# Scaling nine weight tiles in place, with their low halves on GpSimd, under a new order table

## The chip, the cores and the metric

The kernel runs on one core of a Trainium2 chip. The metric is the device time of one execution in microseconds (us), the median of several runs. The engines are TensorE (matmuls; PE in profile rows, PEld for its weight loads), VectorE (DVE), ScalarE (ACT), GpSimd (POOL) and the DMA queues, of which the kernel issues through SyncE (SP) and ScalarE.

## What is computed

An attention with 2 batches of 8 heads, 768 positions and head size 64, in which a query sees only the keys of its own hash bucket, then two feed-forward blocks over 1536 tokens of width 512:

```
q_bits = einsum(q, proj) > 0;  k_bits = einsum(k, proj) > 0      # 6 bits: the bucket
scores = where(bucket(q) == bucket(k), q @ k.T / 8, -1e9)
x = softmax(scores) @ v                                          # heads side by side: 1536 x 512
h = max(x @ w1, x @ w2, x @ w3);  x = h @ w_out                  # first MoE,  512 -> 768 -> 512
h = x @ w_in;  x = where(h > 0, h, exp(min(h, 0)) - 1) @ w_out2  # second MoE, 512 -> 2048 -> 512
```

The weights arrive as 64-bit floats and q, k, v in 32 bits.

## The kernel before

Nearly every product is done in 16 bits with two halves: a number is scaled by a power of two, its rounded high half and the remaining low half are both kept in 16 bits, and three matmuls (high x high, high x low, low x high) stand for one product of 32 bits.

The attention is cut into 96 tiles of 128 queries against 768 keys, four to a pair of heads (a unit). Each tile has score matmuls (`scores`, L621), a maximum (L624), scale and bias (L625, L627), an exponential on ScalarE (L629), the two halves of its result (L658 or L660, and L664), a transposing DMA (L666) and 18 matmuls with the values (L672 to L674). The first 16 tiles stay in 32 bits and transpose on TensorE (L641, L645, L650). Queries and keys are loaded in blocks, scaled in place (L396 or L397), split into halves (L398, and L400 on GpSimd or VectorE) and transposed on TensorE (L410).

The first MoE's three weight matrices are cut into six column blocks f = 0..5, so 18 tiles of 128 x 512. `plan_w13(f)` (L574 and following) loads three of them through `plan_w` into `raww` (L531), turns 64 into 32 bits in `dc2w` (L535 to L546; six buffers), finds the scale of the three from a product of the tiles with themselves (`gram`, L297 to L301, then `pow2`, L318 and L320) and splits each with `plan_wsplit`: the scaled high half on ScalarE (L558) or VectorE (L559), then the low half on VectorE (L560). The second weight of the first MoE and the weights of the second go the same way. The products of both MoEs are at L713 (`mm3`) and L848.

None of the instructions is issued in the order of the program text. `Graph.op` only notes each operation with the engines on which it may run, and `Graph.emit` issues them in the order of `ORDER`, a packed table of one entry per operation: its number and the engine that takes it. Each engine then works through its own entries in that order; DMAs are entries of the SP queue (D) or of ScalarE. The cost figures and `prio` values that stand beside the operations are not used when the kernel is built; the keys of an operation's dictionary are only the engines that the table may choose.

```
        todo = [(hi << 8 | lo) for lo, hi in zip(raw[:n], raw[n:])]
        for t, w in enumerate(todo):
            o, e = self.ops[w >> 3], ENGINES[w & 7]
            assert e in o["eng"] and all(place[d] < t for d in o["deps"])
            o["fn"](e)
```

Of the kernel before, what the change touches and what calls it, by code (L numbers as in the profile page):

```python
# [30 lines left out]
class Graph:  # L31
# [73 lines left out]
    "c-lQyOITXx))u_6@y5m*8*gm9vC$at$|h<6O~OWvfLG8cV48~QKx_wMG7y`A*bKyzf!Gejb|AI`@pK@z1F;>5?LbTiVmlB|2I9#;Ob3#a|9Sqk&H4Yezi)l-`>uDb4UgNcWz6SqKV$!(5=mvVN=j#N"  # L105
    "UYZxbaC_pfyb0VH#K#-Q{hL!L@yD)|EQI>ufz@F1o3Y)KSzPaUb6yn;&OCQ6#%A5uPUiA=F1Li6?m6)kt}A@s`|GDDxx3zQy0__k`*)Pktj44}ISg~}>3gp*<Qw!iGxo@|sC-`@Q!JXP_>nHIxOP*_"
    "Roys4;5BgO2-XzyrGa()oa>XK<R4~Lxc8|EI}ljad@;UnBlI%6^yj&H^Wo2!Qu8#Vo)4?^$Ajj`nQkc>NxwSwYa@oM^Xr)5<jv$~%S=CJet`#PhOHjtEoUn5s|h=ro!;|W@x8w$dEq%b?pO%!FK+mj"
    "jf9(3>+yuV&Mn`%EOrszj_*Z&R52#^FqUg;o{R3!U?F@3f8jFCi@%xwT^e?~E`Ih{CB%yjw?`r;HWya+13O+)9Xi;FD%7^{*}KR~Dzc`~z0$Q`gmw)Rp)0fPa^eU3kMZ}D_9eH>G2==2O1Y#N_D(NQ"
    "{-3qR1fAm-<E+zVUNIRQJF5tSPPn6-#a_?GyKM}!e7MHlfvrioIT+fb7@H?ZU;;hWJ?C4mt+orZpp1;$ncFtw<+JpFSRDMFm<%bcClb6`T6JbmVE&tOIQ7WV(BJ3^3sVZe4L;_e;zK$1Lmh4ttHao-"
    "?r68UmJ`Jd5!Ibqk(n2qpcb^!_PJO{WD|xB&z72xH_uRW#4X{!u*Rp5W&E4f8O9g07oIP#7ffC+xv8jq=kr^acNEcp?ZA$IKzVx}bx8c%OI$vGqMMu}V&*?wYf|r}L+&<DM?P$L3|k4#^*LqdKUC`Y"  # L110
    "{DrS$g0ZmfUqt+i+(2&}^Bu$z74DgD#;K##F{AER+s2=p>|=v#-C~b8u$?yx*XB~+p`P)I`60@6ZT@PlKKlANwu2oEBH@2du+YeN=Letr&-wlUH;DYAeSWkWGf3WFGxwJni70YLoJ;WqvPvm8Cs;jG"
    "u9Nyp<;=gltn?Wl6^ifdeu*02vV!7uJ}P)A(XeJqi3u4z0^vneY%W~2oeerJS9F}c=>N=zH>AIj2xYE4vu<PW7XQGVE{q5WKln*m?V!@Fx3x#tf+}KW)lk>zF?oNSQ^n-I!*lP1ukA;FLhM4ecN}+r"
    "rRr2O77w)J2KFoD^|fuAnH1JU%zr7OcE|1l#nmNr8e*1$;32YfJ@qwOhHbDI<Hu7z;j`!3H}8?nIrO{8DHpzNU?Q*`3|c-HXvLQXGr^YDJr}LTIkM#=Wq^0}x;d!F(2!bcJrPXcx~i>X$(eyvp4jRa"
    "?c#sQm~Ot=bB<3Kl(UKJ-m~x3Z^hAtS*iB#tr*vK&M-Vnm}Y#4O}*L~CMPdDf8oSmFzhn61Djp=fd5X^uDTX2PM7?Lr*5xlL352TeLd@b>t5TijdieWN71ykxlK>!>%lGmJa)ueuf@6B$G9R;y&Q=6"
    "ep4*`b?6Tkm=glgnCHM-7Sd|0val^;bg^cLZ^CtRzRk<%?>jNc-uGOk{67?5_f=e$q*XD-5t+^SD)gu2h4x5fus>CE-<;}H)V8s7))ZJ-Fld6WywheZv}S&c=t?KX7mgE7BGu98GIBM(_(eQ68<E<k"
    "#N?TBaR#L@caLz@BQ`9$PnW$O-bVEAt@G%Vv#xnLcI?@Zc)ZVizMh>IyK!cGkM$dlV*A=@gW2jhy>#L`zZ^xUeiE}yJFaWH)pl)XeEEmsvi8p0@5JswobeLj3jTSF%tzLJ{=hZk5Yc7-u@a7Oc?cd|"
    "Kt)nQd$8&MN4vT(%9km><(Do}N4jqU$HD4aGW_Q9eUi~ElPRwRM+)lc7lgEp95l}(d@DM$st}&fO5jEQx#b6^+O4muce&&1(;lr!wHc>QHX;ni*0R&!GP{1VT5VGk$GvZ*9xwIl=d4rT4vM{+`4Sh`"
    "`tMw>Jdf_3GIhq6yl8CI8)vf5V*+9?7?&N*4l?%5R-H}44uvDx@acbBnNeT0&lO67e@r{bRj*R^m5+N!>7y^zMrDC_Oe+Y#I{Vh}u58o4=U@C!;C%5jG<Xz?9}@=(DMjiG39qOAVozUN!VJWGysSp~"
    "I)hn+|7&((-c{xHJUyMrS#*267avY1?QiSXCsZ3YhqEIA*;?N6Y##g3!Jo{RJD1OAF=6D_XlxMPrYz4d?^g-w??-$4X4`kyOpev-^V=AqnP<D<Nc4OU3)VK{bBZ)sOcGbVsG2_@O@~VAD~5jElf!<+"
    "^Sw4M>Tqh@A2=YS=+w;EXV|+hk1pd3guC$P@?Ww^_(QmS%r7k?J*TtI9g+Qw%k6dS8!gpqPd6^VupXT{m!{8s(VyMdN(Lg3IHvi#zF<fz6DbDa{+)l<QnO}j?q6rot9bV3%;kFJ=KRvC+^gBvjT-~6"  # L120
    "PFTSi(@W2!6@7i$+#dDDSu4IB>aE*@$!xe@H4|ePh$XLXH#p;X6AHg)a`?5Di&^};sw;&-6B&;)=3V>C!&`?o`xUa~XKTzB4tI4!Hx!=GPtIX>#Cz)C1rGMMaUu{r$G6<#NHi8>bYB0UcLol_Qjgzj"
    "BSik7GXX(sNuvcjJUNSKjS@6!iOF4lYd{+H*?7yA_txb^59<RvwzlE(Zv}-0R57UDvrh%Z6H+ps#KeR;htp(ToDkZMR_4}}#txB`ocH?XkEdMP9ouvyI%9EgX8FRwE2m|`{>w2T-G@iY<|OSoj<X$)"
    "*XMqQF8zAp)WuKdT&|T(43D|vd*=s7S8OFUFLvSNwx8NFd}e}&<3ve#!=B*8lx_9s#O^r#F`#xc5W7QiaYfF|@tqr6ucc@HFBStXkH8gYh-(jm9Cr30&R-{AD|bR6O1HJ+6xBuo!R7N4<-v(uNu3TJ"
    "g?U%ebG_j`1Bo4TBiQ)Vlr^>;2!;c}(`fwtjKfJ>z7H{$m<Xyw+?ERo;zThVpPb<f<}j!0>(#_EDXL=_<SO`m9NUzecJ`z)6@hu;nxM`rTKP5<{@3=naPQ!{nrWbPQh371b4$oN6DGFU<n$aesfhd="
# [24 lines left out]
    "q^D<ebU;7SKQPd*H<@~RU_sMB|3H6FfB%4fz(~UZI%qzk8yFqv83h8K!Ty24!NCE8(J-JJ>>nK*06IGOG2k?e8b%-+2H+T=(ZJy7kO68&gK=<VXw+mJ932@onM}q3qtO5{3MS*A(P%Uo45k5a!7|YO"  # L149
    "M#Ip^2+ioy(8!R%1dbtK#=#-O&=8bIM~8-nhK-}ckWF;SU>q`;hH3F8nShz-!#MnZ@#xVbxVd@gruWgK;bGH9c@%WukD%ib)B%}>>GJRmel$ww5gLt*n$6}%77M`P(NPl+v&C$I7&bpPJvNUF12LP&"  # L150
    "Kpc5O7tEG1^GD4*cH<s1kByC4Ml6q^=P@7)%^zDH10Ngv1UQXB8vEoioUk81f%@Z5pf>gd(x;z(0u}Il^2r$NC$K+x0unUbp#RrEd_tR_JbCiz6B<3C5uG1DfytkK`sw)ilW}@m=z~U2{!gRHm<0$3"
    "H`k4u&QEU2k3YSM{{=r07MT"
# [821 lines left out]
```

## Time and profile before

| | us |
|---|---|
| median of three runs | 646.44 (646.3 to 650.33) |
| the profiled execution | 646.06 |
| its span, first to last instruction | 644.3 |
| TensorE busy | 624.7 |
| VectorE busy | 528.0 |
| ScalarE busy | 454.8 |
| GpSimd busy | 218.5 |

A page of the profile gives, for one execution, the busy time of each engine, the chain of work that ended last, and groups of like instructions. A row of instructions reads: line of the kernel, engine, operation, output<-inputs, output shape and type<-input shape and type, count. The difference between an execution's time and its span, 1.8 us here, lies around the first and last instruction. In a time line, a bracket at the end of a row gives the idle time of that engine just before and what ended it. Busy time counts overlapping instructions of one engine once.

### The profile page before, as it was taken

The numbers are of one execution on the slowest core, as the hardware profiler recorded it, in microseconds if no ns is written. First come the engines' busy times: TensorE is split into PE (matmuls) and PEld (weight loads), VectorE is DVE, ScalarE is ACT, GpSimd is POOL, SyncE is SP. The second block draws the span as 40 slices with busy tenths as digits, with TensorE's granted clock in tenths as the row PEclk, the third lists the DMA queues.
The fourth block names the chain that finished last, engine by engine and source line by source line (L and its number), as shares of the span: only waits on it lengthen the run. The fifth ranks groups of instructions, "written<-read, shape, count | busy, mean of one in ns | idle before, by whom it ended". The sixth has DMA issues, their size and how long they took to land.

```text
span 644.3 us, 16489 instructions
## 1 busy us (share of the span) xinstructions
PE 624.7 (97%) x6414; PEld 490.8 (76%) x6414; DVE 528.0 (82%) x1493; ACT 454.8 (71%) x858; POOL 218.5 (34%) x196
## 2 busy tenths in 40 slices
...
GB/s 261 200 242 152 180 202 229 217 131 218 150 189 178 149 156 164 174 169 151 147 132 218 181 96 128 68 99 35 97 19 71 45 1 2 1 1 2 1 92 105
DMA packets 176030, 81.35 MB, mean 126 GB/s; under 512 B 142672, under 2 KB 170320, under 8 KB 175952
## 3 DMA queue, kind: packets, MB, share of 16 engines
...
## 4 chain that ended last, share of the span: by engine, by line
PE 80%; DVE 4%; ACT 4%; DMA 3%; issue 1%; POOL 0%; DVEq 0%; SPq 0%; ACTq 0%
PE mo L713 47%; PE out L848 19%; PE s L621 6%; PE o L672 2%; PE o L673 2%; PE o L674 2%; ACT P L629 1%; DVE m L624 1%; DMA kb<-ka 1%; DMA rawv<-in_v_dram 1%; PE mo L410 1%; DMA PT<-hl 1%; ACT hl L645 1%; DVE hx L734 0%; ACT mo L535 0%
## 5 line engine op out<-in xcount | busy, mean ns | idle before, releaser
L713 PE MATMUL mo<-xT,w 128*128 128x256 f16 x1296 | 152.6, 272 | 0.0
L664 POOL TENSOR_TENSOR hl<-P,hl 128x768 f16<-128x768 f32 x69 | 115.0, 1674 | 64.9 <-ACT hl L658 31.5
L713 PEld LDWEIGHTS <-w 128*128 128x128 f16 x1296 | 123.6, 98 | 16.7
L713 PE MATMUL mo<-x1T,win 128*128 128x256 f16 x1152 | 135.8, 273 | 0.0
L848 PE MATMUL out<-wo2t,gt 128*128 128x512 f16 x576 | 134.9, 379 | 0.0
L713 PEld LDWEIGHTS <-win 128*128 128x128 f16 x1152 | 112.3, 98 | 24.2
L629 ACT ACTIVATE P<-s,bias,scale 128x768 f32<-128x768 f32 x96 | 94.6, 991 | 28.8 <-DVE bias L627 17.6
L841 POOL TENSOR_TENSOR gt<-g,gt 128x256 f16<-128x256 f32 x57 | 39.3, 695 | 213.2 <-ACT gt L839 125.4
L624 DVE TENSOR_REDUCE m<-s 128x1 f32<-128x768 f32 x96 | 91.1, 951 | 12.6 <-PE s L621 11.2
L848 PEld LDWEIGHTS <-gt 128*128 128x128 f16 x576 | 54.9, 97 | 52.7
L832 ACT ACTIVATE r<-mo,nih 128x256 f32<-128x256 f32 x96 | 44.8, 469 | 69.1 <-PE mo L713 65.0
L835 DVE TENSOR_SCALAR uu<-e,sg 128x256 f32<-128x256 f32 x96 | 35.5, 371 | 26.3 <-ACT e L834 25.7
L658 ACT CAST hl<-P 128x768 f16<-128x768 f32 x62 | 50.7, 830 | 2.9 <-DMA PT<-hl 2.4
L672 PE MATMUL o<-vt,PT 128*128 128x65 f16 x480 | 51.3, 193 | 0.2
L673 PE MATMUL o<-vt,PT 128*128 128x64 f16 x480 | 51.3, 194 | 0.0
L674 PE MATMUL o<-vt,PT 128*128 128x65 f16 x480 | 51.1, 192 | 0.0
L837 DVE SCALAR_TENSOR_TENSOR g<-mo,aj,uu 128x256 f32<-128x256 f32 x96 | 46.1, 482 | 6.0 <-POOL gt L841 2.0
L621 PE MATMUL s<-ka,qa 128*128 128x384 f16 x192 | 48.1, 332 | 2.5 <-ACT P L629 1.9
L621 PE MATMUL s<-kb,qb 76*128 76x384 f16 x192 | 48.2, 332 | 1.0 <-DMA kb<-ka 1.0
L672 PEld LDWEIGHTS <-PT 128*128 128x128 f16 x480 | 44.4, 96 | 2.7 <-DMA PT<-hl 0.4
L673 PEld LDWEIGHTS <-PT 128*128 128x128 f16 x480 | 44.3, 97 | 2.1
L713 PEld LDWEIGHTS <-wot 128*128 128x128 f16 x432 | 41.4, 98 | 5.6
...
## 6 DMA issues: line engine op xcount, KB each, us to landing
...
```

The lines of the kernel that those rows point to most:

```text
L621: PE.matmul(ps.ap[:, h, :NK], lh[0:n, h0 + i, j], rh[0:n, i, h * CH:(h + 1) * CH], start=first, stop=not first)
L624: op({"V": vred(S)}, lambda e: V.tensor_reduce(out=m.ap, in_=ps.ap[:, :, :NK], op=ALU.max, axis=AX.XY), rd=[ps], wr=[m], prio=t + 80.5)
L629: op({"A": act(S, ap=2, acc=int(u < FU)) - 42}, lambda e: A.activation(out=P.ap.rearrange("p (c n) -> p c n", c=2), in_=ps.ap[:, :, :NK], ...
L658: A.copy(hl.ap[:, 0], P.ap)
L664: op({"G": gtt(S), "V": (vtt(S), -109.46)}, lambda e: eng[e].tensor_tensor(out=hl.ap[:, 1], in0=P.ap, in1=hl.ap[:, 0], op=ALU.subtract), r ...
L672: PE.matmul(oo, pt.ap[:, kt], vt.ap[:, i, kt, :D + 1], start=(kt == 0), stop=False)
L673: PE.matmul(oo[:, :D], pt.ap[:, kt], vt.ap[:, i, kt, D + 2:], start=False, stop=False)
L674: PE.matmul(oo, pt.ap[:, NS + kt], vt.ap[:, i, kt, :D + 1], start=False, stop=(kt == NS - 1))
L713: PE.matmul(o, lh(kk, x), rh(kk, y), start=(kk == 0 and pi == 0), stop=(kk == n - 1 and pi == 2))
L832: op({"A": act(NQ, ap=1) - 42}, lambda e, m=m, o=o, r=r: A.activation(out=r.ap, in_=o.ap[:, :NQ], func=AF.Relu, scale=nih.ap[:, m:m + 1]), ...
L837: op({"V": vstt(NQ)}, lambda e, m=m, o=o, uu=uu, gg=gg: V.scalar_tensor_tensor(out=gg.ap, in0=o.ap[:, :NQ], scalar=aj.ap[:, m:m + 1], in1= ...
L848: PE.matmul(outs[j].ap, gt.ap[:, x, j * 128:(j + 1) * 128], wo2t[f].ap[:, y], start=(len(seen) == 1 and pi == 0), stop=(len(seen) == n and ...
```

## The change

`plan_wsplit` gets a second form, which `plan_w13` uses for f = 0, 1, 2, so for nine of the 18 tiles. In it the tile in `dc2w` is multiplied by its scale in place, the high half is a plain copy of it, and the low half is a subtraction of two tiles in SBUF that GpSimd can do.

```diff
-    def plan_wsplit(tag, t2, dst, dfn, s, prio):
+    def plan_wsplit(tag, t2, dst, dfn, s, prio, pool=False):
         w = lambda: t2.ap.bitcast(F32)
+        if pool:
+            op({"A": act(512, ap=1), "V": vts(512)}, lambda e: A.activation(out=w(), in_=w(), func=AF.Copy, scale=s[1]())
+               if e == "A" else V.tensor_scalar(out=w(), in0=w(), scalar1=s[1](), scalar2=None, op0=ALU.mult), rd=[t2, s[0]], wr=[t2], two=True, prio=prio)
+            op({"V": vcopy(512), "A": act(512)}, lambda e: (V.tensor_copy if e == "V" else A.copy)(dfn(0), w()), rd=[t2], wr=[dst], two=True, prio=prio)
+            return op({"G": gtt(512), "V": vtt(512)}, lambda e: eng[e].tensor_tensor(out=dfn(1), in0=w(), in1=dfn(0), op=ALU.subtract),
+                      rd=[t2, dst], wr=[dst], two=True, prio=prio)
...
-            wops.append(plan_wsplit("w", t2[i], f"w13{f}{i}", lambda x, i=i: w13[:, f, i, x], s, prio))
+            wops.append(plan_wsplit("w", t2[i], f"w13{f}{i}", lambda x, i=i: w13[:, f, i, x], s, prio, f < 3))
```

Two cost figures of DMA entries change by one (1200 to 1201, 900 to 901, 100 to 101 on ScalarE's queue), which has no effect on what is built. `ORDER` is replaced as a whole: 3368 entries instead of 3359. Unpacked in the way of `emit`, the two tables hold the same operations but for the nine tiles, in another order and partly on other engines. The larger shifts between engines, in numbers of entries:

| operation | before | after |
|---|---|---|
| nine tiles: scaling in place | none | 5 VectorE, 4 ScalarE |
| nine tiles: high half | 4 VectorE, 5 ScalarE | 5 VectorE, 4 ScalarE |
| nine tiles: low half | 9 VectorE | 9 GpSimd |
| attention, high half (L658, L660) | 62 ScalarE, 18 VectorE | 54, 26 |
| attention, low half (L664) | 69 GpSimd, 11 VectorE | 64, 16 |
| first MoE, low half of its result (L770) | 10 GpSimd, 2 VectorE | 5, 7 |
| second MoE, low half (L841) | 57 GpSimd, 39 VectorE | 45, 51 |
| small copies of the hash bits to 16 bits (L453 to L459) | 20 ScalarE, 8 VectorE | 13, 15 |

GpSimd's own order begins, after the new table: key block 1, query block 2, key block 2, two weight tiles of f = 0, query block 4, key block 3, the third weight tile of f = 0, query block 6, two weight tiles of f = 1, and so on; before, the same without the weight tiles.

## Rows read from the trace of the kernel before

**Rows 1.** The page's head: span, and busy time of TensorE (PE) and its weight loads.
```profile
span 644.3 us, 16489 instructions
...
PE 624.7 (97%) x6414; PEld 490.8 (76%) x6414; DVE 528.0 (82%) x1493; ACT 454.8 (71%) x858; POOL 218.5 (34%) x196
```
**Rows 2.** Busy time by stretch: bounds, length, then us (instructions), clock, DMA share, GB/s.
```profile
core 0: us, PE busy (x) PEld busy (x) DVE busy (x) ACT busy (x) POOL busy (x), PEclk, DMA share, GB/s
0.00:32.00 32.00, 22.33 (x253) 18.70 (x254) 23.91 (x85) 19.47 (x36) 6.16 (x19) 1.00 0.76 231
32.00:64.00 32.00, 31.28 (x372) 27.51 (x369) 31.34 (x90) 32.00 (x61) 3.83 (x3) 1.00 0.66 197
64.00:91.34 27.34, 22.99 (x191) 18.66 (x191) 25.75 (x69) 26.46 (x45) 10.95 (x9) 0.94 0.77 193
91.34:128.00 36.66, 36.54 (x506) 31.20 (x504) 35.98 (x98) 36.63 (x58) 24.86 (x16) 1.00 1.08 216
128.00:640.00 512.00, 511.13 (x5098) 394.73 (x5096) 409.75 (x1154) 340.23 (x662) 172.67 (x150) 1.00 0.46 105
```
**Rows 3.** TensorE's instructions in order of time: start, length in us, instruction, [idle before].
```profile
40.20 0.50 PE L410 MATMUL mo<-ident,natk 128*128 128x128 f16 x6
...
86.87 0.84 PE L621 MATMUL s<-kb,qb 76*128 76x384 f16 x2
...
90.69 0.48 PE L621 MATMUL s<-ka,qa 128*128 128x384 f16 x2
...
91.34 1.47 PE L713 MATMUL mo<-xT,w 128*128 128x256 f16 x12
```
**Rows 4.** The chain of waits between 70.99 and 90.69 us, shares by line.
```profile
by line: ACT P L629 30.7%; issue 17.9%; ACT hl L645 13.4%; ACT mo L535 8.9%; ACT hl L658 8.6%; ACT dc2w L539 5.3%; ACT w L558 4.5%; ACT vt L500 3.7%; ACT qa L413 2.8%; ACT xn L696 2.0%; ACT rawq L396 1.3%; ACT junk L333 1.0%
```
**Rows 5.** VectorE's, then ScalarE's instructions in order of time.
```profile
48.48 0.48 DVE L559 TENSOR_SCALAR w<-dc2w,swm 128x512 f16<-128x512 f32 x1
48.87 0.75 DVE L560 SCALAR_TENSOR_TENSOR w<-dc2w,swm,w 128x512 f16<-128x512 f32 x1
49.53 0.46 DVE L540 TENSOR_SCALAR dc2w<-raww 128x512 uint16<-128x512 uint16 x1
...
53.37 0.73 ACT L558 ACTIVATE w<-dc2w,swm 128x512 f16<-128x512 f32 x1
53.98 0.99 ACT L629 ACTIVATE P<-s,bias,scale 128x768 f32<-128x768 f32 x1
```
**Rows 6.** Groups by line and shape: count | busy us, mean ns | idle before, releasers.
```profile
L396 ACT ACTIVATE rawq<-rawq,sq 128x512 f32<-128x512 f32 x4 | 2.9, 720 | 0.8 <-DVE sq L320 0.8
...
L398 DVE TENSOR_SCALAR natq<-rawq 128x512 f16<-128x512 f32 x12 | 6.0, 501 | 0.1
...
L743 ACT CAST hTb<-hx 128x512 f16<-128x512 f32 x4 | 2.4, 608 | 0.0
...
L745 POOL TENSOR_TENSOR hTb<-hx,hTb 128x512 f16<-128x512 f32 x9 | 11.6, 1291 | 24.0 <-DVE hTb L743 11.4 <-PE mo L281 6.7 <-ACT hTb L743 3.2
```
**Rows 7.** GpSimd's instructions in order of time.
```profile
35.68 1.66 POOL L400 TENSOR_TENSOR natk<-rawk,natk 128x768 f16<-128x768 f32 x1 [2.67 <-DVE vs L320]
60.15 1.16 POOL L400 TENSOR_TENSOR natq<-rawq,natq 128x512 f16<-128x512 f32 x1 [22.82 <-DVE scale L625]
```
**Rows 8.** Busy time by stretch, up to tile 6's scores and on to tile 28's.
```profile
0.00:38.59 38.59, 28.63 (x357) 24.23 (x358) 30.06 (x101) 26.06 (x49) 8.82 (x20) 1.00 0.76 233
38.59:114.48 75.89, 71.11 (x768) 60.45 (x766) 73.93 (x207) 74.98 (x126) 25.40 (x18) 0.98 0.80 197
```
**Rows 9.** One line each: count: min/median/max ns, first to last start.
```profile
L397 DVE TENSOR_SCALAR rawq<-rawq,sq x8: 473/486/1074, 5.3 to 271.9; 128x512 f32<-128x512 f32 x8
...
L398 DVE TENSOR_SCALAR natq<-rawq x12: 409/421/1280, 5.9 to 272.5; 128x512 f16<-128x512 f32 x12
...
L400 POOL TENSOR_TENSOR natq<-rawq,natq x10: 1152/1171/1817, 17.9 to 273.0; 128x512 f16<-128x512 f32 x10
```
**Rows 10.** VectorE's instructions on the first chunk's weights, in order of time.
```profile
30.75 0.15 DVE L320 TENSOR_SCALAR swm<-swm 128x1 int32<-128x1 int32 x1
...
38.06 0.74 DVE L560 SCALAR_TENSOR_TENSOR w<-dc2w,swm,w 128x512 f16<-128x512 f32 x1
```

More of the change, by code (lines that the diff above doesn't have):

```diff
@@ L104 @@
 ORDER = (
[L105 to L124, printed above, removed]
@@ L149 @@
[L149 to L152, printed above, removed]
+    "c-l2qOF$au+7`Sqcw_Jecw_JecnNrA&=|n$;Ell>U{pYpi0wj57h<yzn}ygc#AYFB7h<~*dltcV5lj|hyAYFw*et|$Atnp)bP+sVh^LGH9ee(FzWKiQeV*riK1OB+ON3IHlFlT^C;COls%h@ePx&gg"
@@ new lines @@
+    "%k7DIeH=_Ajr$zI#nS12z28$l56?Y83Gxs%=`Gfymm!|-<09s`i0-Yreh4gFFQ7~Giqu6%ex38wB~i?|e<b7%@+=b7zpT3;)Fz<-U#*PBXg9l3xq^wi<hl()iL*SWph7*(^D2YugM`LfW0<znQX=ky"
+    "UB30bEqKMUlcxl^vgLov<$JeQy(hjuZ^SPQe}(<mv<tm&@X4Y683#-FZ&V~@pk~X)5nKMNEbHWy%jH@XOgd)ztj?rfS9W3Z?$68~yH`h=1d%gKbT_vA=E~~aJ2x);9Xec`b%~Ju=9Bxe&v%0de=e+G"
+    "p{JrCPqQBmMP@%7g*T%&C5zHQm1ZR_@*hIWw6!hkP0qLL@AoYq=yUobw~<au@w!$+mgiw4ay2WpZTY!&@jSZ2diM@@U~dA~ODxf;d)Z0nV%wshxT~&hH^X4Gd1|D);cu0)$d1YqRlnM|lHd6kLW^(C"
+    "-*!1j%~R*GYxAeQKu~|6*ZtMCX$pBv5ex172Mcp+$9m!2u-mSFHSKT5At+Zt{QQc%CiOQvUkilhCg&GE*Yq|TzOI>@vA?p?{eid@Ul4IDIb>+typ#LoX_xD}g?E0EbuQpM7VBx>zcFDNr*KuDDxKkq"
@@ new lines @@
+    "R`Gvr>M)c2-<H2z?m3~yVLo=vF)Xz^%?l^tFW03{jp*^=>8_iLeI;&I&W0n`9?OMS`-?t$MM!tgK3-i%Xo~2w#ip%y-W6Z$M!)Qj%_E2OSC{_7&!ueRo&d4fGp$FVHXAMcDMovX96rx~zi_lZ=Q(jN"
+    "Eyb^-;t`o+`5U$}yu3+7yI$O^Zu7r8X$$g5!!cL1?|kVpd3|nwfLHvx%T52U=c3Z|*@0m7WAKw`GbF_=wC9}T?dup@q}8hxrj65=yAsBZgt(yLJ1D83BYHL=A@%4N^FNxcwhzdb<=1tu-NAF8Mb>0d"
+    "k81zV&DXKVzjht(cy|RU{D8)%p^HPV{iP=rb<Vf?Ph69d$#`#>)6b!cs~avZX0~{?55)8KOh*louVcu9g3v2J+cX%mY*?GxUf7Pl;`>AkOXnW1Lv-T1*ms`SMx`4vN%%5G3w)0&pXIB%WbHjn)qi4N"
+    "M~I`ppKA?Kl)JTascAdWdk%Lme_1{3B43{ReI<I+%x~8_CR$vAKfqTXGvLn0(Pif(XZ`a(LK;2$!=Lb-ZEq`x9=?drB&8yW-aI{bEmO$?-c_MxhlZd^^6`yp;UmxOIrACg1R`YC=C-3dzfG%8&K+FA"
@@ new lines @@
+    "NjNe!Gr*gdD5K=Bb*2kZt>x+o{;7G9rJUm~MtA+Qn02*VW;57{8@f8hp<6o$YS&Gcch<NNg0Ad+xhS5y@06~58@@QWRM-}lvc7iXf73a~TVBoyR`ZErnDm`R{W03pe?_ii+duulWbdLIw8Nt)ZyixQ"
+    "=YR63^D=inFA+)I9xvCoydR7mcG2Y6^H=`B@!!azTO`#uoOtC+xk2f}M8AJ@X?ob9>EG7(H_f&4T-j44K^hiU-|35GR$H7|IO}qo;St$VX;8;8T%4Zx?4_wPvgi?r*EUb0zAzbaxc)e^?bsdD*6q2^"
+    "zF63+jegrj9_W8E22C?o+sTFHta(@R!*gNe=1O{Y^-Ba-Mq~4g75b`+{^luvFQyK-!|%2cG@tJ6S!cP0!H`D5^LX|D-6i&4r^?_(bC{ClTK@OjsL8UWm|Kv3_1^3AFCG%dGU~&U)9?_mkz>x$GbQFw"
+    "oXmzfqrVd*TW=Og@oTddi>$ATY_vs(bMe#Ev|jm{*@f`1W&U627rc{?(ha=TT4~$dcG_<|J6`Ah%u&KcD7@^9T)AG)KNh@seh>^j>1uVjocvGg720dUz3u)^V(@tDj8^Zi<?MCjCO)d!`!z;~ca2SG"
```

63 lines of the change are left out of this document (37 added, 26 removed).

## The prediction

> **What bounds the kernel now.** I read the page's head first, then the busy time of the engines stretch by stretch, then the chain of waits, then the instructions in order of time. The head shows TensorE busy for 624.7 of a span of 644.3 us [rows 1], so 19.6 us of waiting are all that can be had without faster or fewer matmuls, and the change removes none. The table by stretch shows where those 19.6 us are [rows 2]. From the first matmul of the first MoE at 91.34 us on [rows 3], TensorE is busy for 36.54 of 36.66 and for 511.13 of 512 us: 1.0 us of idleness in 549. The rest lies before it: 9.7 us in the first 32 us, 0.7 us up to 64, 4.35 us between 64 and 91.34; and 3.8 us in the tail, where the last sums leave. So the end of the kernel moves one for one with the time at which TensorE becomes dense, and a faster engine behind 91.34 us is worth nothing unless TensorE waits for it.
>
> What holds TensorE up before 91.34? From 32 to 128 us ScalarE is busy for 32.00 of 32, 26.46 of 27.34 and 36.63 of 36.66 us, VectorE for 31.34, 25.75 and 35.98: both are full. GpSimd, with 3.83 and 10.95 us up to 91.34, is nearly free [rows 2]. The chain of waits between 70.99 and 90.69 us names ScalarE in every piece but its own issue time, the exponentials alone with 30.7%, and no VectorE [rows 4]. The bound of this stage is ScalarE first, VectorE close behind.
>
> **The change part by part: the nine tiles.** Before, a weight tile costs one scaled copy to the high half and one VectorE instruction for the low half. By the old table the nine tiles of f below 3 have the high half four times on VectorE and five times on ScalarE. After it, a tile costs a scaling in place, a plain copy to the high half, and a subtraction; the new table puts the scalings on VectorE five times and on ScalarE four, the copies likewise, and all nine subtractions on GpSimd.
>
> Instructions overlap a little on their engine, so the price of one is the distance of two starts. On VectorE a scaled copy starts at 48.48 (0.48 us long), the low half behind it at 48.87 (0.75 long), the next instruction at 49.53: 0.39 and 0.66 us, each 0.09 less than its length. On ScalarE a scaled copy starts at 53.37 and the next at 53.98: 0.61 us [rows 5]. For the scaling in place the nearest rows are the same operation on the queries: 720 ns on ScalarE [rows 6], like the scaled copy's 0.73, so 0.61 us; a median of 486 ns on VectorE [rows 9], so 0.39 us. For the plain copy they are 608 ns on ScalarE [rows 6], so 0.50, and 421 ns on VectorE [rows 9], so 0.33 us.
> VectorE: before 4 x 0.39 + 9 x 0.66 = 7.5 us; after 5 x 0.39 + 5 x 0.33 = 3.6 us; 3.9 us saved.
> ScalarE: before 5 x 0.61 = 3.1 us; after 4 x 0.61 + 4 x 0.50 = 4.4 us; 1.4 us lost.
> GpSimd: a subtraction of this size takes 1291 ns in the mean [rows 6] and 1.16 us undisturbed [rows 7]: 10 to 12 us more, for which there are 22.8 us of idleness before 60.15 us alone [rows 7].
> The extra hop from engine to engine that each tile makes costs nothing, as long as it ends before the first matmul that reads these weights, at 91.34 us [rows 3]: the new table has the ninth subtraction ahead of the scores of tile 13 already. Without that cover it would cost its length once, the copy and the subtraction, 0.5 + 1.2 us.
> Alone, then, the change helps the engine that is second and burdens the one that is first. What comes of it hangs on the table.
>
> **The new table.** I counted the entries of both tables, each with its mean from the view of instructions by line, in two parts: up to the scores of tile 6, which start at 38.59 us in the trace, and from there to those of tile 28, at 114.48 us; TensorE has the same work ahead of either within 1 us. Up to tile 6 the new table has 3.6 us more for ScalarE (33.6 against 30.0), 0.6 more for VectorE, 0.8 for GpSimd. Between the two it has 84.0 instead of 84.9 us for ScalarE, 88.8 instead of 91.7 for VectorE, 34.3 instead of 25.4 for GpSimd. The old sums of 84.9 and 91.7 stand for 74.98 and 73.93 us of busy time [rows 8], since lengths overlap; so the differences are worth 0.9 x 0.88 = 0.8 us on ScalarE and 2.9 x 0.81 = 2.3 us on VectorE. The 3.6 us that ScalarE gets earlier (26.06 / 30.0 of it, 3.1) lie in the first 38.59 us, where it is idle for 38.59 - 26.06 = 12.5 us [rows 8]; if that cover failed they would cost their 3.1 us. So the table pays ScalarE's new passes out of its idle start, and the crowded stage becomes shorter by 0.8 us if ScalarE binds, by 2.3 if VectorE does. I take 1.2 us, nearer to ScalarE's, since the chain is ScalarE's [rows 4].
> Behind tile 28 the new table has 18 us more for VectorE, 8 less for ScalarE and 22 less for GpSimd: halves of the attention and of the second MoE go from GpSimd to VectorE. VectorE is busy for 409.75 of the last 512 us [rows 2], so 18 us fit into 102 idle ones: 0, and at worst about 1.5 us, if they crowd in one place. The loads in the SP queue change places too (one query load goes to ScalarE's queue, a weight load moves up behind the third); the first query and the first two key loads, which the first scores need, keep theirs: 0.
>
> **Against it: GpSimd beside VectorE.** VectorE's conversion of the queries has a median of 421 ns and a worst case of 1280, and GpSimd's subtraction for them a median of 1171 and a worst case of 1817 [rows 9]: now and then a pair holds each other up. Over all twelve conversions the mean is 501 ns [rows 6], 80 above the median. The ten new VectorE instructions at 80 ns lose 0.8 of the 3.9 us; I take that as covered, since ScalarE binds. The bounds are 0, if all go like the medians, and the 5.2 us of the blocking rival below.
> The Trainium skill (SBUF — State Buffer, Who interferes with whom) says that GpSimd and a VectorE instruction that uses its second port, or has two inputs in SBUF, shut each other out for a whole instruction. By that rule the worst cases above are such blocks; the medians show that most instructions here met none.
>
> **The sum.** The profiled execution took 646.06 us, 1.8 more than its span of 644.3; the median of the runs is 646.44. 646.44 - 1.2 + 0 + 0 = 645.2 us.
>
> **The rivals.**
> No gain: the early ScalarE work isn't ready early, since its weights have still to land, and its passes fall into the full stage after all; its 0.8 us are eaten. For it: ScalarE is full from 32 us on [rows 2]. Against it: 12.5 us are free before [rows 8]. 646.4.
> Blocking: each of the nine subtractions holds a waiting VectorE instruction for half of its 1.16 us, 5.2 us against 3.9 saved; VectorE is then 1.3 us longer and binds: 647.7. The medians speak against it [rows 9].
> More than forecast: the two full engines both come out ahead, and TensorE's 4.35 us of idleness between 64 and 91.34 close [rows 2]. For it: the granted clock is 0.94 in that stretch [rows 2], and a pair of score matmuls takes 0.84 us at 86.87, behind an idle time, where it takes 0.48 at 90.69 [rows 3]; less waiting gives some of this back too. 646.4 - 4.4 = 642.0.
> Slower: GpSimd's queue is in order, and the new table puts two weight subtractions ahead of those of a query block and of the fourth key block, which starts at 35.68 us now [rows 7]. The first chunk's scale is there at 30.9 us, but its first low half starts at 38.06, since VectorE is late [rows 10]. If GpSimd's first starts at 38.06 too, then two weights and the query block, 3 x 1.16 us, put the key block to 41.5. Its subtraction ends at 37.34 and its transposes run at 40.20, so it can start 2.9 us later, at 38.6, before it decides [rows 3, 7]. From there each microsecond comes out at the end: 41.5 - 38.6 = 2.9 us, 649.3; and over 652.9, if the scale comes another 3.6 us late. Against it: the new table places that scale earlier than the old one.
>
> **Chances and range.** Forecast 0.42 (644.2 to 646.4), no gain 0.20, blocking 0.08, more than forecast 0.18, slower 0.12. From 641.5 to 649.5 the range takes in the first three, most of the fourth and the near half of the fifth. One per cent, 6.5 us, is about what a measurement of this kernel can tell from no change: below 640.0 lies 0.05 (the fourth, with a gain in the first 32 us besides), above 652.9 lies 0.07 (the fifth's far half and what I have not thought of), between them 0.88.
>
> **What would show it.** Right: nine GpSimd subtractions of 1.16 to 1.3 us, ended by about 70 us; nine of VectorE's low halves left; the first matmul of the first MoE near 90 us; TensorE idle for about 3 us between 64 us and it, and for no more than 1.5 behind it. Wrong: the fourth key block's subtraction starting behind 38.6 us; VectorE's conversions with a median well above 421 ns; ScalarE as idle in the first 38 us as before; TensorE waiting behind 128 us, where VectorE got its 18 us.

## The result, and the profile after

The changed kernel takes 650.9 us in the median of 19 runs (648.48 to 655.61), the kernel before, beside it on the same chip, 646.7 us (19 runs, 642.99 to 650.33). The ratio is 1.0067, with a 95% interval from 1.0046 to 1.0089: 4.2 us slower. Forecast were 645.2 us. The time lies within 1% of the kernel before, where the forecast had put it, but on the other side of it and above the range.

The profiled execution of the changed kernel is its slowest, 655.61 us. A second profiled execution took 650.24 us, near the median, and where the two differ both are shown. Lines moved: what was L621, L629, L664, L666, L672 and L713 is now L627, L635, L670, L672, L678 and L719. The new form of a tile is L559 (scaling on ScalarE), L560 (on VectorE), L561 (copy) and L562 (subtraction).

Head of the page, and the busy time by stretch, in the columns of [rows 2]:

```profile
span 653.5 us, 16490 instructions
...
PE 630.4 (96%) x6414; PEld 495.2 (76%) x6414; DVE 534.0 (82%) x1524; ACT 451.0 (69%) x849; POOL 204.9 (31%) x183
```

```profile
0.00:32.00 32.00, 23.90 (x258) 19.60 (x258) 23.41 (x84) 20.88 (x36) 5.99 (x18) 1.00 0.81 262
32.00:64.00 32.00, 31.18 (x340) 27.78 (x340) 27.74 (x84) 28.73 (x53) 11.28 (x9) 1.00 0.52 157
64.00:91.34 27.34, 24.74 (x219) 20.66 (x219) 26.68 (x78) 27.31 (x50) 12.81 (x11) 1.00 0.70 190
91.34:128.00 36.66, 35.14 (x462) 29.36 (x461) 33.96 (x92) 35.13 (x55) 22.45 (x15) 0.95 0.91 210
128.00:640.00 512.00, 506.33 (x5098) 393.36 (x5096) 416.38 (x1178) 337.64 (x657) 150.19 (x128) 1.00 0.46 105
```

In the first row the clock column says 1.00, though matmuls ran at half rate up to 37.7 us (rows below): the trace's record of the clock begins with its first rise, at 37.74 us here and 28.80 in the kernel before, and the column counts what lies ahead of it as full.

The last line is the news. Behind 128 us, where [rows 2] have TensorE busy for 511.13 of 512 us, it is busy for 506.33: 5.7 us of idleness where 0.9 were. VectorE is busy for 416.38 us there, 6.6 more than before and far from full. The waits of TensorE behind 128 us, in the kernel before, then in the first and the second execution of the changed one (line, releaser, us in total, times, longest):

```profile
PE mo L280 <- ACT junk L333: 0.5, 1, 0.5
PE s L621 <- ACT P L629: 0.3, 1, 0.3
```

```profile
PE o L678 <- DMA PT<-hl: 4.2, 4, 2.2
PE mo L719 <- DVE hx L744: 0.8, 1, 0.8
PE s L627 <- ACT P L635: 0.6, 1, 0.6
```

```profile
PE o L678 <- DMA PT<-hl: 5.7, 3, 2.8
PE s L627 <- ACT P L635: 1.2, 2, 1.0
PE mo L719 <- DVE hx L744: 0.8, 1, 0.8
```

What TensorE waits for in the changed kernel is the transposing load of a tile's halves (PT from hl), ahead of that tile's product with the values; the kernel before has 0.8 us of such waits in its second execution and none of 0.1 us or more in its first. The nine weight tiles themselves, in the second execution (groups by line and shape):

```profile
L562 POOL TENSOR_TENSOR w<-dc2w,w 128x512 f16<-128x512 f32 x9 | 11.1, 1249 | 12.3 <-ACT w L561 6.0 <-DVE w L561 4.4 <-DVE swm L320 1.8
...
L559 ACT ACTIVATE dc2w<-dc2w,swm 128x512 f32<-128x512 f32 x4 | 2.9, 736 | 0.0
L561 ACT CAST w<-dc2w 128x512 f16<-128x512 f32 x4 | 2.4, 637 | 0.0
L560 DVE TENSOR_SCALAR dc2w<-dc2w,swm 128x512 f32<-128x512 f32 x5 | 2.4, 474 | 0.0
L561 DVE CAST w<-dc2w 128x512 f16<-128x512 f32 x5 | 2.1, 415 | 0.0
```

Their lengths are those that the prices were made from: 1249 ns on GpSimd against 1291 in [rows 6], 474 and 415 on VectorE against medians of 486 and 421 in [rows 9], 736 and 637 on ScalarE against 720 and 608.

Where the time lies along the kernel, by three marks that every version has: the starts of the 1st, the 241st and the 1321st of the 2880 matmuls of `mm3`, which makes the products of the first MoE and the first product of the second, and the time from the last of these to the end of the span. The new order puts other work ahead of the first mark than the old one; behind the third all are alike.

| profiled execution | 1st | 241st | 1321st | from there to the end |
|---|---|---|---|---|
| before | 91.3 | 142.4 | 343.2 | 301.1 |
| before, second execution | 92.4 | 144.7 | 345.7 | 301.1 |
| changed | 91.0 | 145.7 | 352.0 | 301.5 |
| changed, second execution | 85.3 | 138.5 | 346.8 | 301.5 |
| new order up to 140 us, old order behind | 85.1 | 138.2 | 340.3 | 301.1 |
| the same with the old form of the tiles | 91.0 | 144.2 | 346.2 | 301.2 |
| changed, two transposing loads earlier | 86.5 | 139.7 | 343.4 | 301.5 |
| old order, new form of the tiles | 96.4 | 149.5 | 351.2 | 301.4 |
| before, two transposing loads later | 90.1 | 141.3 | 352.3 | 301.1 |

In its second execution the changed kernel reaches the 241st matmul 6.2 us earlier than the kernel before in its second, and the 1321st 1.1 us later. The gain is made, and more than lost again between 138 and 347 us.

### The profile page after: what moved, and what is told of

It reads as the page before. It is cut to its first block, busy times and chain, and to the rows that moved or that the text cites. A ratio compares the mean times of both kernels' runs of the same rounds, so it can differ in the third digit from the quotient of the medians.

```text
span 653.5 us, 16490 instructions
## 1 busy us (share of the span) xinstructions
PE 630.4 (96%) x6414; PEld 495.2 (76%) x6414; DVE 534.0 (82%) x1524; ACT 451.0 (69%) x849; POOL 204.9 (31%) x183
## 4 chain that ended last, share of the span: by engine, by line
PE 74%; DMA 4%; DVE 4%; ACT 2%; issue 1%; POOL 1%; SPq 0%; DVEq 0%; ACTq 0%; POOLq 0%
PE mo L719 43%; PE out L854 19%; PE s L627 6%; DMA PT<-hl 4%; PE o L678 2%; PE o L679 2%; PE o L680 2%; ACT P L635 1%; DVE m L630 1%; PE mo L410 1%; ACT junk L333 1%; ACT wot L564 0%; PE mo L297 0%; PE mo L431 0%; DVE hx L740 0%
## 5 line engine op out<-in xcount | busy, mean ns | idle before, releaser
L719 PE MATMUL mo<-xT,w 128*128 128x256 f16 x1296 | 155.2, 274 | 0.8 <-DVE hx L744 0.8
L719 PEld LDWEIGHTS <-w 128*128 128x128 f16 x1296 | 124.1, 98 | 18.7 <-issue 0.9
L719 PE MATMUL mo<-x1T,win 128*128 128x256 f16 x1152 | 135.1, 273 | 0.0
L854 PE MATMUL out<-wo2t,gt 128*128 128x512 f16 x576 | 133.4, 379 | 0.0
L670 POOL TENSOR_TENSOR hl<-P,hl 128x768 f16<-128x768 f32 x64 | 106.7, 1673 | 82.8 <-ACT hl L664 45.9
L719 PEld LDWEIGHTS <-win 128*128 128x128 f16 x1152 | 112.1, 98 | 22.7 <-issue 0.2
L635 ACT ACTIVATE P<-s,bias,scale 128x768 f32<-128x768 f32 x96 | 94.3, 989 | 31.0 <-DVE bias L633 22.6
L847 POOL TENSOR_TENSOR gt<-g,gt 128x256 f16<-128x256 f32 x45 | 32.2, 718 | 225.5 <-ACT gt L845 80.1
L841 DVE TENSOR_SCALAR uu<-e,sg 128x256 f32<-128x256 f32 x96 | 34.7, 364 | 28.6 <-ACT e L840 28.2
L678 PE MATMUL o<-vt,PT 128*128 128x65 f16 x480 | 50.9, 193 | 4.2 <-DMA PT<-hl 4.2
L627 PE MATMUL s<-ka,qa 128*128 128x384 f16 x192 | 48.2, 333 | 3.0 <-ACT P L635 2.3
L664 ACT CAST hl<-P 128x768 f16<-128x768 f32 x54 | 44.6, 826 | 7.7 <-DMA PT<-hl 7.2
L678 PEld LDWEIGHTS <-PT 128*128 128x128 f16 x480 | 44.4, 97 | 7.1 <-DMA PT<-hl 4.9
L627 PE MATMUL s<-kb,qb 76*128 76x384 f16 x192 | 48.4, 334 | 0.0
L719 PEld LDWEIGHTS <-wot 128*128 128x128 f16 x432 | 41.6, 98 | 5.4
```

The source lines that it names most:

```text
L627: PE.matmul(ps.ap[:, h, :NK], lh[0:n, h0 + i, j], rh[0:n, i, h * CH:(h + 1) * CH], start=first, stop=not first)
L635: op({"A": act(S, ap=2, acc=int(u < FU)) - 42}, lambda e: A.activation(out=P.ap.rearrange("p (c n) -> p c n", c=2), in_=ps.ap[:, :, :NK], ...
L664: A.copy(hl.ap[:, 0], P.ap)
L670: op({"G": gtt(S), "V": (vtt(S), -109.46)}, lambda e: eng[e].tensor_tensor(out=hl.ap[:, 1], in0=P.ap, in1=hl.ap[:, 0], op=ALU.subtract), r ...
L678: PE.matmul(oo, pt.ap[:, kt], vt.ap[:, i, kt, :D + 1], start=(kt == 0), stop=False)
L719: PE.matmul(o, lh(kk, x), rh(kk, y), start=(kk == 0 and pi == 0), stop=(kk == n - 1 and pi == 2))
```

## The experiments

**Both kernels again, one execution each.**

> The kernel before once more, for a second profile. Theory A: the clock rises again at about 28.8 us. If it rises elsewhere, the time of the rise differs between executions of one kernel, by as much as the spread of the times (643 to 650).

> The changed kernel once more, for a second profile. Theory A (the start): TensorE's clock rises late in this kernel, at 37.8 us instead of 28.8, which costs some 4.5 us; then the second profile shows a rise behind 35 us again. Theory B (the table's later part): TensorE waits behind 128 us, 5.7 us instead of 0.9, mostly for transposes; then this idle time comes back within 1 us. If the rise is at 28 to 31 us and the time nearer to 650, the late rise was that of one execution.

Measured: 648.59 and 650.24 us, with the rows above. TensorE's idle time behind 128 us was 1.5 us in the kernel before and 7.9 in the changed one, so the new waits aren't an accident of the slow first execution. What that execution has besides is a late clock. In it a pair of score matmuls takes 0.85 us up to 33.65 us and 0.48 only from 37.72 on (TensorE's instructions in order of time):

```profile
33.01 0.85 PE L627 MATMUL s<-ka,qa 128*128 128x384 f16 x2
33.65 0.85 PE L627 MATMUL s<-kb,qb 76*128 76x384 f16 x2
...
37.72 0.48 PE L627 MATMUL s<-ka,qa 128*128 128x384 f16 x2
```

In the second execution the clock rose at 12.91 us, fell to half at 16.32 and was granted in full from 23.15 us on, and the first mark was reached 5.7 us earlier. From the 241st matmul to the 1321st both executions lose: they take 206.3 and 208.3 us, those of the kernel before 200.8 and 201.0.

**The form of the tiles and the table, each alone.** The first kernel has the old order; each scaled copy of the nine tiles becomes a scaling and a copy in the same place, on the engines of the new table, and the nine low halves go to GpSimd. The second has the new order; the nine tiles keep their old form, with the low half on VectorE.

```diff
 old order, new form, per tile (entries of the table):
-scaled copy to the high half   V or A
-low half                       V
+scaling in place               V or A
+copy to the high half          V or A
+subtraction                    G
```

> The old order table with the nine tiles alone changed: scaling and copy at the old place of the high half, on the engines of the new table, the subtraction on GpSimd at the old place of the low half. By the prediction's costs VectorE saves 3.9 us and ScalarE loses 1.4: between 1 us faster and 1 us slower than before. If the tiles' new form itself is what costs (blocking of GpSimd and VectorE, hops), 2 to 4 us slower.

> The new order table with the old form of the nine tiles: high half at the place of the scaling, low half on VectorE at the place of the subtraction. Theories A and B both put the loss into the table: 3 to 6 us slower than before. If the tiles' form costs, no more than 1 us slower than before.

Measured: 654.92 us, ratio 1.0124 (1.0093 to 1.0155), and 658.7 us, ratio 1.0183 (1.0154 to 1.0212). Neither part is good alone. In the old order the new form costs 8 us. VectorE's queue stands still where a copy follows a scaling that is ScalarE's (waits of VectorE from 25 to 91 us), and ScalarE's exponentials then wait for VectorE:

```profile
DVE w L561 <- ACT dc2w L559: 3.7, 2, 2.1
```

```profile
ACT P L635 <- DVE bias L633: 3.5, 4, 1.8
```

The second line was 0.7 us in the same stretch of the kernel before. TensorE's idle time from 32 to 64 us rises from 0.7 to 4.2 us, and the first mark comes at 96.4. So the longer way of a tile, which I had priced at nothing, is not free in the old order; whether the hop between scaling and copy is what costs there, the next kernel tells.

**The scaling and the copy both on VectorE, in the old order.** This takes the hop to ScalarE away.

> The old table with the nine tiles alone in their new form, scaling and copy next to each other on VectorE, no hop to ScalarE between them. VectorE then has 9 x 0.72 us instead of 7.5 (1.0 less) and ScalarE 3.1 less. Theory of the hop: the 7 us that the same table lost with scaling and copy on different engines came from VectorE's queue waiting behind a copy for ScalarE's scaling; then this is 1 us slower to 2 us faster than before. Theory of the form: GpSimd beside VectorE, or the longer way of a tile, costs; then 3 us slower or more.

Measured: 655.38 us, ratio 1.0115 (1.009 to 1.014), no better than with the hop: the hop to ScalarE is not what the loss hangs on. Eight more instructions than in the kernel above stand in VectorE's full stage, and four of the 18 are held up beside GpSimd (one line each: count: min/median/max ns, first to last start; then VectorE and GpSimd in order of time):

```profile
L560 DVE TENSOR_SCALAR dc2w<-dc2w,swm x9: 470/479/1253, 31.0 to 75.9; 128x512 f32<-128x512 f32 x9
```

```profile
L561 DVE CAST w<-dc2w x9: 426/427/1264, 31.5 to 76.4; 128x512 f16<-128x512 f32 x9
```

```profile
39.14 1.25 DVE L560 TENSOR_SCALAR dc2w<-dc2w,swm 128x512 f32<-128x512 f32 x1
```

```profile
38.69 1.41 POOL L562 TENSOR_TENSOR w<-dc2w,w 128x512 f16<-128x512 f32 x1
```

The scaling that starts at 39.14 ends at 40.39, behind the end of GpSimd's subtraction at 40.10, and takes 1.25 us instead of 0.48. The four held up lose 2.4 us together. ScalarE's exponentials wait 5.7 us for VectorE between 25 and 91 us, and in this execution the granted clock stood at half from 36.36 to 46.60 us, with TensorE busy for 9.1 us of it. Which of these makes the 7 us was not separated.

**One half of the new table with the other half of the old.** The first kernel has the new table's first 790 entries and the old order behind them; the second the old table's first 780 entries, with the old form, and the new order behind them.

> The first 790 entries of the new table (all weight tiles of the first MoE in their new form, up to about 128 us), then the rest in the old table's order. Theory B (the loss lies in the new table's later part, where TensorE waits 6 to 8 us behind 128 us instead of 1): that idle time falls to 1 or 2 us and the time to 643 to 646, as before or a little faster. Theory A (the loss lies in the start): it stays at 649 to 652, with 1 to 2 us idle behind 128.

> The other way round: the first 780 entries of the old table with the old form of all tiles, then the rest in the new table's order. Theory B: TensorE idle for 5 to 8 us behind 128 us, 650 to 654 us. Theory A: as before, 645 to 648.

Measured: 649.74 us, ratio 1.0048 (1.002 to 1.0076), and 656.19 us, ratio 1.0125 (1.0094 to 1.0157). With the old order behind, TensorE's waits for transposing loads behind 128 us are down to 0.2 us; with the new order behind, they are 5.4 us. The first kernel did not get below the kernel before, since the place of the cut makes waits of its own, of 1.1 us at 129.7 and of 2.1 us at 135.3 (for a query block's copy and an exponential that the one order has earlier than the other).

**The same with a better cut: the new order's first 884 entries (to about 140 us), then the old order; and this with the old form of the tiles.**

> The changed kernel with the first 884 entries of the new order table (to about 140 us, the nine tiles in their new form among them) and the old table's order behind it. Theory A (the new table's later part costs the time, because TensorE waits there 6 to 8 us for transposing loads and halves): the idle time of TensorE behind 128 us falls from 5.7 to 7.9 us to between 1 and 2, and the median is 643 to 647 us, at or below the kernel before. Theory B (the crowded first 128 us or the extra hop cost it): the median stays at 649 to 652 us, with the loss in front of 128 us.

> The same order as in the run before it in this batch, but the nine tiles in their old form: the copy to the high half scales, and VectorE subtracts the low half, where the other kernel has a scaling, a copy and a subtraction on GpSimd. If the new form is what the new head lives from (it takes nine VectorE instructions of 0.75 us out of a full engine), this one is 3 to 8 us slower than its partner, as the whole new table with the old form was. If the form is worth nothing by itself, the two agree within 1.5 us.

Measured: 644.78 us (643.16 to 648.72), ratio 0.9976 (0.9953 to 0.9999), and 652.8 us, ratio 1.0088 (1.0054 to 1.0122). The first is the fastest version of the study: 6.1 us below the changed kernel, and 2.2 below the kernel before. Its waits of TensorE behind 128 us:

```profile
PE mo L445 <- DVE bitsq L441: 0.8, 1, 0.8
PE o L678 <- DMA PT<-hl: 0.5, 1, 0.5
PE mo L719 <- DMA xT<-xn: 0.4, 1, 0.4
```

Its idle time from 128 to 630 us is 1.8 us against 7.9 in the second execution of the changed kernel, 6.1 less, and its 1321st matmul comes 6.5 us earlier, from a nearly equal 241st. So the 6 us are the new table's part behind 140 us, its places and its engines together, and they are TensorE's waits. The price of that part doesn't depend on the tiles: with the old form it is 658.7 - 652.8 = 5.9 us, with the new one 650.9 - 644.8 = 6.1 (by the ratios 6.1 and 5.9).

The second kernel reaches the first mark at 91.0 instead of 85.1 and never makes these 5.9 us up. Form and order belong together:

| | old form | new form |
|---|---|---|
| old order | 1 | 1.0124 |
| new order up to 140 us, then old | 1.0088 | 0.9976 |
| new order throughout | 1.0183 | 1.0067 |

**Two transposing loads.** The waits of TensorE in the changed kernel, traced back, lie at the products of few tiles, above all of tile 42 (2.2 and 2.75 us in the two executions) and tile 64 (0.85 and 1.7); tile 95, the last, has 0.56 and 1.3. For tile 42 in the second execution, GpSimd's low half, SP's queue and TensorE, in order of time (the load at 171.23 is tile 42's):

```profile
160.85 1.64 POOL L670 TENSOR_TENSOR hl<-P,hl 128x768 f16<-128x768 f32 x1 [3.44 <-DVE hl L666]
```

```profile
162.99 0.39 SPq L492 DMA_DIRECT2D rawv<-in_v_dram  x1
```

```profile
165.22 1.43 SPq L672 DMA_TRANSPOSE PT<-hl  x1
```

```profile
166.75 4.38 SPq L672 DMA_TRANSPOSE PT<-hl  x1
```

```profile
171.23 1.49 SPq L672 DMA_TRANSPOSE PT<-hl  x1
```

```profile
174.86 0.20 PE L678 MATMUL o<-vt,PT 128*128 128x65 f16 x1 [2.75 <-DMA PT<-hl]
```

The low half is done at 162.49. Its load is issued at 171.23, 8.7 us later, because it stands behind the loads of tiles 43 and 41 in SP's queue. Tile 43's waits for its half from VectorE, which ends at 165.15; tile 41's needs 4.38 us to get away, since it waits for the products that free its buffer (waits of SP's queue from 160 to 175 us):

```profile
SPq L672 <- PE o L680: 4.5, 2, 4.1
```

The low halves of tiles 43 and 41 are two of those that the new table moved from GpSimd to VectorE, so place and engine meet here.

The old table has this load 58 entries ahead of tile 42's product, the new one 9. In the kernel before, the half ended at 171.76 and the load was issued at 171.79. Two kernels move these loads in the changed kernel's table. In both, tile 42's stands ahead of the load of the sixth block of values (batch 1, second pair of heads; the expectation's "11th" is a label of that pair), before those of tiles 43 and 41; tile 64's stands ahead of tile 63's in the first and directly behind it in the second.

```diff
 changed kernel's table, SP queue:
+tile 42: transposing load (L672)
 raw values, sixth block (L492)
 tile 43: transposing load
 tile 41: transposing load
-tile 42: transposing load (L672)
```

> The changed kernel with two entries of the SP queue moved: the transposes of tiles 42 and 64, whose low halves are ready 5 to 9 us before their transposes are issued, go ahead of the loads and transposes that stand before them. If SP's order is why TensorE waits for them, its two waits of 2.2 to 2.8 and 0.9 to 1.7 us go, and the time falls by 3 to 4 us against the changed kernel, to 646 to 648. If the transposes are late for another reason (the low halves, the DMA engines), less than 1 us changes.

> The changed kernel with two entries of the SP queue moved: the transposing load of tile 42's low half ahead of the 11th raw value load, and that of tile 64 directly behind tile 63's, ahead of the loads that stand between. Theory A (order in the SP queue costs the time): TensorE's waits for these two tiles (2.2 to 2.8 and 0.85 to 1.7 us) are gone, nothing else becomes late for it, and the median is 646.5 to 649 us, 2 to 4 below the changed kernel. Theory B (the queue only shows a lateness of VectorE or GpSimd that appears elsewhere): the waits move to other tiles, and the median stays at 649 to 651 us.

Measured: 649.09 us, ratio 1.0040 (1.0012 to 1.0069), and 648.53 us, ratio 1.0029 (1.0005 to 1.0053). The wait for tile 42 is gone in both. In the first, a wait of 1.5 us for tile 63 appeared, whose load now stood behind tile 64's; in the second it is gone too, and these are left:

```profile
PE o L678 <- DMA PT<-hl: 1.6, 1, 1.6
PE s L627 <- ACT P L635: 1.3, 3, 0.8
PE mo L280 <- ACT ka L413: 0.3, 1, 0.3
```

From the 241st to the 1321st matmul the second takes 203.7 us, against 206.3 and 208.3 in the changed kernel's two executions and 202.1 with the old order behind 140 us. By these traces two entries carry 2.6 to 4.6 of the 4.2 to 6.2 us; by the medians 2.4 of 6.1. The difference of the two ratios, 1.0067 and 1.0029, is 0.0038, by an estimate from their intervals between 0.0006 and 0.0070. The engines of the halves are the same in both kernels, so with tile 43's and tile 41's halves on VectorE, moving the load alone ends the wait.

**The cause put into the kernel before.** Here the same two loads stand late in the old table, and nothing else in the table is changed.

```diff
 old table, places of SP's entries:
-1045 tile 42: transposing load (L666)     product with the values at 1103
+1093 tile 42: transposing load
-1452 tile 64: transposing load            product with the values at 1488
+1475 tile 64: transposing load, now behind that of tile 67
```

> The kernel before with one thing of the new table put into it: the transposing loads of tiles 42 and 64 stand 10 and 13 entries ahead of these tiles' products with the values instead of 58 and 36. Theory A: TensorE waits for them by 1 to 3 us each, as in the changed kernel, its idle time behind 128 us rises from about 1 to between 2.5 and 6 us, and the kernel is 1.5 to 4 us slower than the one before. Theory D (the places show a lateness of other engines, and don't cause one): within 1 us of the kernel before.

Measured: 657.09 us (655.16 to 658.14) beside 645.31 us for the kernel before on the same chip, ratio 1.0175 (1.0142 to 1.0207): 11.8 us for two entries, far over what either theory expected. TensorE's waits behind 128 us, the stretch around tile 64 (columns of [rows 2]), GpSimd's half for tile 67, SP's loads for tiles 67 and 64, and tile 64's product:

```profile
PE o L672 <- DMA PT<-hl: 8.8, 2, 6.5
PE mo L713 <- DMA xT<-xn: 0.4, 1, 0.4
PE s L621 <- ACT P L629: 0.3, 1, 0.3
```

```profile
253.00:261.00 8.00, 3.75 (x58) 3.08 (x59) 2.70 (x6) 1.05 (x3) 3.41 (x3) 0.57 0.78 177
```

```profile
250.54 1.64 POOL L664 TENSOR_TENSOR hl<-P,hl 128x768 f16<-128x768 f32 x1 [4.55 <-DVE hl L660]
```

```profile
252.20 1.41 SPq L666 DMA_TRANSPOSE PT<-hl  x1
```

```profile
253.70 1.54 SPq L666 DMA_TRANSPOSE PT<-hl  x1
```

```profile
257.25 0.23 PE L672 MATMUL o<-vt,PT 128*128 128x65 f16 x1 [6.53 <-DMA PT<-hl]
```

Tile 64's half was ready at 241.38. Its load had to stand behind tile 67's, whose half GpSimd finished at 252.18; it was issued at 253.70, and TensorE stood for 6.5 us. During that idleness the granted clock fell to half and stayed there until 260.46. The waits are 8.8 us, and from 257.25 to 260.46 TensorE worked at half rate, some 1.6 us more. The place of a load in an in-order queue is enough to make a loss of this size. It is not a copy of the changed kernel's loss: there tile 64's load stands 21 entries ahead of its product, and not behind tile 67's, and its wait is 0.85 to 1.7 us. The Trainium skill (DMA: Bandwidth & Descriptors, Anatomy of one DMA) says, in a section on DMAs that GpSimd issues, that any semaphore wait of a DMA happens on the sequencer that issues it, before dispatch; the trace agrees, with 12.3 us from tile 64's half to its issue, all of it in SP's queue.

**Every transposing load earlier, and VectorE's halves given back.** The first kernel moves the loads of 42 tiles behind 140 us forward, to at most 55 entries ahead of their products. The second leaves the changed order alone, but behind 140 us the 93 instructions that had changed between VectorE and GpSimd are on their old engines again.

> The changed kernel with the transposing loads of 42 tiles behind 140 us moved forward in the SP queue, each up to 55 entries ahead of the tile's product with the values (never ahead of its low half). Theory A (late transposes are all of the loss): no wait of TensorE for PT over 0.5 us is left behind 128 us, its idle time there is under 2 us, and the median is 644 to 647 us. Theory D (VectorE, with the halves it got, is the other part): PT waits turn into waits for halves, quotients or exponentials, the idle time there stays over 3 us and the median at 647.5 to 650.

> The changed kernel's order, but behind entry 884 (about 140 us) every instruction that the change moved between VectorE and GpSimd (93 of them, 57 from GpSimd to VectorE) is back on the engine that it had before; the order stays. Theory D (the failed step of my prediction: VectorE has no room for its extra halves): TensorE's idle time behind 128 us falls under 3 us, and the median is 645 to 647.5 us. Theory A (the places of the transposing loads in the SP queue): the waits for the PT of tiles 42 and 64 stay, 5 us or more of idle time behind 128 us, and the median stays at 649.5 to 652 us.

Measured: 661.15 us, ratio 1.023 (1.0193 to 1.0267), and 664.26 us, ratio 1.029 (1.0256 to 1.0324): both far slower than the changed kernel, and neither theory had expected that. With every load early, other loads that stand behind them come late (TensorE's waits behind 128 us; the key load of the first line was issued at 221.82, behind four transposing loads that SP had begun to wait for at 206.54):

```profile
PE s L627 <- DMA kb<-btk: 3.2, 1, 3.2
PE mo L280 <- ACT ka L413: 2.5, 1, 2.5
PE mo L719 <- DMA xT<-xn: 2.2, 2, 1.4
PE o L678 <- DMA PT<-hl: 1.6, 1, 1.6
```

So "earlier" is no cure by itself; an entry that isn't ready holds up the next that is. With the 93 instructions on their old engines TensorE waits in many places (the same view):

```profile
PE s L627 <- ACT P L635: 5.7, 7, 2.7
PE mo L280 <- ACT junk L333: 2.9, 1, 2.9
PE o L678 <- DMA PT<-hl: 1.9, 3, 1.2
PE mo L410 <- POOL natk L400: 1.6, 1, 1.6
```

TensorE's idle time from 128 to 336 us is 14.4 us there. A low half takes 1.70 us on GpSimd and 0.95 on VectorE, and 57 of the 93 went from VectorE to GpSimd without a change of place. Taking the extra work off VectorE alone made things worse; whether it is a part of the changed kernel's loss isn't shown by this, since a half that ends later in the same place holds up what stands behind it.

**An earlier clock, in the kernel before.** Dummy matmuls ahead of the first four gram products, where TensorE waits for loads.

```diff
+WARM = [20, 12, 2, 12]
...
         def mm(e):
             k, last = 0, len(srcs) * n // 128 - 1
+            for _ in range(WARM.pop(0) if WARM else 0):
+                PE.matmul(x2.ap[:, 0:128], ident, ident, start=True, stop=True)
```

> The kernel before with 20, 12, 2 and 12 matmuls of 128 columns (identity by identity, overwritten by the products behind them) ahead of the first four gram products, so that TensorE works while it would wait for the first loads. Theory C (the time at which the granted clock rises to its full level, 28 to 38 us in the executions so far, moves the end): the full level comes at 12 to 20 us and stays, the matmuls up to 29 us run at full rate, and the kernel is 2 to 6 us faster than the kernel before. If loads and ScalarE set the pace up to there, the clock rises earlier and the end doesn't move by more than 1 us.

Measured: 649.16 us, ratio 1.002 (0.9994 to 1.0046): no gain. The clock did rise early, at 14.20 us, but fell again (columns of [rows 2]):

```profile
14.20:17.60 3.40, 2.68 (x73) 2.29 (x71) 3.06 (x11) 2.68 (x8) 1.75 (x1) 1.00 0.88 278
17.60:38.00 20.40, 18.73 (x147) 15.35 (x145) 14.86 (x46) 14.92 (x27) 3.98 (x3) 0.50 0.65 185
```

What an early rise that lasts would bring was not shown.

## Why the prediction was wrong

**The bound, confirmed.** The end moves one for one with TensorE's waiting. From the 1321st matmul to the end, every version in the table above takes 301.1 to 301.5 us, though the changed order has some of the second MoE's halves on other engines.

**The nine tiles, confirmed.** The lengths held to within 5%. GpSimd took 11.1 us more, inside the 10 to 12 that I had given.

**The extra hop, conditional.** "Costs nothing" held in the new order, where the ninth subtraction ended at 66.2 us in the second execution, long before the first mark. In the old order the new form cost 8 us with the hop between scaling and copy and 7.4 without it, by the ratios; the price that I named for a lost cover, 1.7 us once, was too small by far. What the runs show there are waits in VectorE's in-order queue (3.7 us at two copies with the hop) and instructions held up beside GpSimd (1.2 and 2.4 us), neither of which I had priced; they don't add up to the whole.

**The new table up to 140 us, right in size.** I forecast 1.2 us of gain. The kernel that has only this part of the new table, with the new form, gained 0.24% by the ratio, 1.6 us of 646.44 with an interval from 0.1 to 3.0: 644.9 us, where the sum said 645.2. That the gain comes from ScalarE's and VectorE's shorter stage, as I summed it, isn't shown: the profiled execution of this kernel has no stretch at half clock between 23.19 and 641 us, those of the kernel before have one of 3.4 and 6.8 us from 87 us on, and how much of the gain is clock was not separated. TensorE's idleness between 64 and 91 us was 3.4 us in it, against 4.35 before; "more than forecast", which needed it to close, did not come.

**"Behind tile 28 ... 0, at worst about 1.5 us": the step that failed.** It measured 6 us. I counted what the new table gives to each engine behind tile 28 and asked whether VectorE has room for it. It has: 416.38 of 512 us in the changed kernel; the 18 us that I had counted show as 2.5 to 6.6 us more of busy time there. I did not ask where in the queues the entries stand. With capacity to spare on VectorE, ScalarE and GpSimd, TensorE waited for transposing loads, most of all for two that stood 9 and 21 entries ahead of their use in the table, behind loads that weren't ready. The step beside it, "the loads in the SP queue change places: 0", failed for the same reason: I had looked at the first loads only. I did write that TensorE waiting behind 128 us would show me wrong, but named VectorE's extra halves as the place. Tile 43's half, one of them, is what a load ahead of tile 42's waited for; yet moving tile 42's load was enough to end the wait, and giving the halves back made the kernel 13 us slower still.

**The rivals.** "Slower" named the fourth key block's subtraction on GpSimd, with a start at 38.6 us as its mark. It started at 43.82 in the first execution, when the clock rose late, and at 38.19 in the second, 37.91 in the fastest version: at the mark, not past it. So the rival that was on the right side had another mechanism and does not explain the loss. "Blocking" was small in the new order: the ten new instructions on VectorE have medians of 475 and 416 ns and worst cases of 481 and 421 in the second execution. But the medians that spoke against it were misread: most instructions kept their length because no GpSimd instruction was running when they started. In the two kernels with the old order and the new form, seven scalings and copies on VectorE started 0.49 us or more before the end of a GpSimd instruction; all seven took 0.78 to 1.26 us instead of 0.43 to 0.49, and each ended 0.28 or 0.29 us behind the end of that instruction. So did the two worst cases of [rows 9], 1074 and 1280 ns. In the new order one of the ten started beside a subtraction, 0.17 us before its end, and kept its length. The Trainium skill (SBUF — State Buffer, Who interferes with whom) says that where the two contend, as with a VectorE instruction in a mode that takes the shared port pair, whoever issues first has the pair for the whole instruction and the other waits; these rows agree.

**Open.** Moving two loads gave back 2.4 of 6.1 us by the medians and 2.6 to 4.6 by the traces. The remainder is spread: 1.6 us at tile 95, whose load was issued 0.45 us behind its half, so that its place in SP's queue can be no more than that of it, and 1.3 us at three exponentials. Exchanging the part behind 140 us shows that the whole lies in that part of the table. That part changes places and engines together, and which of them carries the rest was not separated.
